# Retention and mixture of experts on one core: slot tables read ahead of weight pieces, squares moved up, later weight pieces issued around the second expert's column reads

## The chip, the cores and the metric

The kernel runs on one core of one Trainium2 chip. The metric is device time in microseconds (us) of one execution; lower is better. The kernel before takes 409.28 us, the median of 3 runs (408.39 to 411.97).

## What is computed

Two layers, one after the other. The first is a retention layer over 4 batches, 8 heads, 768 steps and 64 channels per head; the second routes each of the 3072 resulting rows of 512 numbers to one of 8 experts, a two-layer network with 1024 hidden units, and scales the result by the row's gate.

```python
for t in range(S):
    state = gamma[None, :, None, None] * state + np.einsum('bhd,bhe->bhde', k[:, :, t], v[:, :, t])
    y[:, :, t] = scale * np.einsum('bhd,bhde->bhe', q[:, :, t], state)
...
expert_idx = np.argmax(logits, axis=1)
...
h = np.maximum(x[mask] @ w1[e], 0.0)
out[mask] = gate_w[mask, None] * (h @ w2[e])
```

## The kernel before

The retention layer is worked in 12 blocks of 256 steps (12 is `NM`), and its rows go to DRAM (`xd`). For each row the routing picks an expert and a rank in it, and an indirect DMA on POOL writes the row's number, token and logits into that place of a slot table in DRAM (`tbl`, line 566). An expert works on the first rows of its part of the table: 416 rows for expert 0, down to 356 for the eighth (`CAPS`).

**Expert 0 starts before routing is finished.** Its first 288 slots, the early rows, are filled by block 8, so they are gathered (`xge`) and run through the first layer while the last blocks are still being placed. The other 128 slots, the late rows, can be read only when the last scatter of the slot table has landed: SP reads the slots (line 945, `tb[:, 0, 3]`), POOL gathers the rows they name (`xr0`, line 596), and TensorE turns them (line 1100). SP also reads the 512 slots of experts 1 and 2 (`slots`, line 913), for which it must first have the expert's number in a register (`load_expert`, line 178, a load of `cnti`).

**The rows of expert 1** take the long way that all later experts take: gathered by POOL in four indirect DMAs (`gather_rows`, line 596), written to DRAM by SP (`write_rows`: three DMAs of line 982 and one of line 986, each behind its own gather), and read back by columns in four DMAs (`read_quarters`, line 1001, `xg`; here called the column reads; 832 KB in all), which wait until all four writes have landed. DVE transposes what was read (`x_turn`, line 1011), ACT casts it to a high part, and DVE subtracts to get the low part (`x_low`, line 1018). TensorE needs both for expert 1's first layer (line 237).

**Weights come in pieces** of 512 KB, eight for each expert: four of the first layer's matrix (line 194), four of the second's (line 198). Piece g is loaded by `load_piece` into one of four buffers `raw`, so its load waits until piece g-4 has been split. `split` has ACT cast the piece to a high part `whi` (line 219) and DVE subtract to get the low part `wlo` (line 224). Every matrix product is done three times, high by high, high by low and low by high. Pieces 8 to 11 are the first layer of expert 1, pieces 12 to 15 its second layer. They are split in this order: piece 8 after the third tile of expert 0's second layer, 9 between the two halves of the late rows' first layer, 10 and 11 each behind one of the two turns of the late rows' hidden units (`turn_hidden`, lines 1138 and 1139).

**What sets the order.** Every engine works through its instructions in the order in which the program is written, and so does SP, whose queue carries all direct DMAs: an issue that waits holds up every issue behind it. `square` (line 278, ACT) sums the squares of a block of 128 rows for the gates. The POOL memset of `xr0` (line 1086) reuses memory of `xge`, so it waits for the squares of the early rows.

Of the kernel before, what the change touches and what calls it, by code (L numbers as in the profile page):

```python
# [32 lines left out]
NE = 8  # L33
# [6 lines left out]
CAPS = (416, 408, 400, 392, 384, 380, 360, 356)  # L40
# [5 lines left out]
EARLY = 288  # L46
EROWS = ((0, P), (1, P), (2, EARLY - 2 * P))
# [58 lines left out]
def retention_moe(ctx: ExitStack, tc: tile.TileContext, q, k, v, emb, tau, w1, w2, const, const16, out):  # L106
    nc = tc.nc
# [17 lines left out]
    tbl = dp.tile([NE * STRIDE, SW], F32, name="tbl")  # L125
# [12 lines left out]
    tb = cp.tile([P, NE, NG, 2 + NE], F32, name="tb")  # L138
# [35 lines left out]
    def after(i, o):  # L174
        tc.add_manual_dep(i.ins, o.ins.name, SYNC, reason="pace")

    def load_expert(s):
        expert[s] = nc.values_load(cnti[:, s:s + 1], engines=(ET.SP,), min_val=0, max_val=NE - 1)

    def load_piece(behind=None):  # L180
        g = nload[0]
        if g >= NPC:
            return
        nload[0] += 1
        s, j = divmod(g, 8)
        e = expert[s]
        r = rp.tile([P, 1024], F32, name="raw")
        if s == 0 and j < 4:

            for jj in range(KT):  # L190
                f = P * jj + Q * j
                nc.sync.dma_start(out=r[jj * Q:(jj + 1) * Q], in_=w1[0, f:f + Q, :])
        elif j < 4:
            i = nc.sync.dma_start(out=r, in_=w1r[ds(e * DM + j * P, P), :])
            if behind is not None:
                after(i, behind)
        else:
            i = nc.sync.dma_start(
                out=r.rearrange("p (c d) -> p c d", c=2),
                in_=w2r[ds(e * DF + 2 * (j - 4) * P, 2 * P), :].rearrange("(c p) d -> p c d", p=P))  # L200
            if behind is not None:
                after(i, behind)
        raw_t[g] = r

    def split_cast(parts=1):

        g = nsplit[0]
        if g >= NPC:
            return lambda *a: None
        nsplit[0] += 1  # L210
        r = raw_t.pop(g)
        hi = wp.tile([P, 1024], F32R, name="whi")
        lo = wp.tile([P, 1024], F32R, name="wlo")
        views = [t.rearrange("p (q t a) -> p q t a", q=8, t=4) for t in (r, hi, lo)]
        if g % 8 >= 4 and g // 8 not in ROWS:
            views[1:] = [t.rearrange("p (t q a) -> p q t a", q=8, t=4) for t in (hi, lo)]
        vs = [tuple(t[:, i * 8 // parts:(i + 1) * 8 // parts] for t in views) for i in range(parts)]
        for rv, hv, _ in vs:
            nc.scalar.copy(out=hv, in_=rv)  # L219
        piece[g] = (hi, lo)  # L220

        def low(*engs):
            for eng, (rv, hv, lv) in zip(engs or (nc.vector,) * parts, vs):
                eng.tensor_tensor(out=lv, in0=rv, in1=hv.bitcast(F32), op=ALU.subtract)  # L224
        return low

    def split(*engs):
        split_cast(len(engs) or 1)(*engs)
# [47 lines left out]
    def square(xr, n, j, at, e=0):  # L276
        sq = cp.tile([P, DM], BF16, name="sq")
        nc.scalar.activation(out=sq[:n], in_=xr[:n, j], func=AF.Square, accum_out=ssqs[e % 2][:n, at:at + 1])  # L278
# [39 lines left out]
    xge = ap_.tile([P, len(EROWS), DM], F32, name="xge", bufs=1)  # L318
# [442 lines left out]
    for m in range(NM):  # L761
# [16 lines left out]
        n = 2 if m < 7 else 3 if m < 8 else 4  # L778
# [44 lines left out]
        else:  # L823
# [6 lines left out]
            if m == 2:  # L830
                after(nc.sync.dma_start(
                    out=tbl.rearrange("(e s) c -> e (s c)", e=NE)[:, :FILL * SW].rearrange("e (p x) -> e p x", p=P // NE),
                    in_=none), i)
# [72 lines left out]
    def run(n):  # L906
        for _ in range(n):
            next(todo, None)

    def slots(e):  # L910
        if e not in expert:
            load_expert(e)
        nc.sync.dma_start(out=tb[:, e], in_=tbl[ds(expert[e] * STRIDE, NG * P), :2 + NE].rearrange("(j p) o -> p j o", p=P))
# [19 lines left out]
    for o in held:  # L933
        o()
    low()
    for _ in range(9):
        next(sort_steps)
        run(1)
    load_expert(1)
    load_piece()  # L940
    run(10)
    split()
    load_piece()
    load_expert(2)
    nc.sync.dma_start(out=tb[:, 0, 3], in_=tbl[EARLY:CAPS[0], :2 + NE])
    slots(1)
    slots(2)
    run(12)
    split()
    for j, n in EROWS:  # L950
        square(xge, n, j, j)
    run(12)
    split()
    load_piece()
    load_piece()
    run(DF)
    ctxa.close()
    turn_of[:] = ["b2", "b3"]
# [16 lines left out]
    def full_rest(e):  # L975
        return divmod(blocks_of(e) * Q, P)

    def write_rows(e):
        full, rest = full_rest(e)
        xr, xs = xrs[e], xsd[e % 2]  # L980
        for j in range(full if e == 1 else 0):
            nc.sync.dma_start(out=xs[j * P:(j + 1) * P], in_=xr[:, j])
        if e > 1:
            nc.sync.dma_start(out=xs[:full * P].rearrange("(j p) x -> p j x", p=P), in_=xr[:, :full])
        if rest:
            nc.sync.dma_start(out=xs[full * P:full * P + rest], in_=xr[:rest, full])

    def squares(e, part=None):
        full, rest = full_rest(e)
        sizes = [(j, P) for j in range(full)] + [(full, rest)] * (rest > 0)  # L990
        for j, n in sizes if part is None else sizes[2 * part:2 * part + 2]:
            square(xrs[e], n, j, j, e)
# [4 lines left out]
    def read_quarters(e):  # L997
        nb, xs = blocks_of(e), xsd[e % 2]
        xg = xgs[e] = mp.tile([P, NXC, P], F32, name="xg")
        for i in range(NQ):  # L1000
            nc.sync.dma_start(out=xg[i * Q:(i + 1) * Q, :nb],
                              in_=xs[:nb * Q, i * P:(i + 1) * P].rearrange("(n b) x -> b n x", b=Q))
# [3 lines left out]
    def x_turn(e, kt):  # L1006
        if kt == 0:
            xTs[e] = (hp.tile([P, KT, CAP], F32R, name="xh"), hp.tile([P, KT, CAP], F32R, name="xl"))
        xt = xts[e, kt] = mp.tile([P, NXC, Q], F32, name="xt", bufs=2)
        n = blocks_of(e)  # L1010
        nc.vector.transpose(out=xt[:, :n], in_=xgs[e][:, :n, kt * Q:(kt + 1) * Q])  # L1011
        nc.scalar.copy(out=xTs[e][0][:, kt, :CAPS[e]], in_=xt.rearrange("p n b -> p (n b)")[:, :CAPS[e]])  # L1012
# [98 lines left out]
    gsteps = gates(0, [(n, slice(j, j + 1), tb[:n, 0, j:j + 1, 2:]) for j, n in (*EROWS, (3, P))])  # L1111
    next(gsteps)
    write_rows(1)
    hr = mp.tile([P, DF], F32, name="hr")
    for f in (slice(0, 512), slice(512, 1024)):
        acc = acc_()
        n = 0
# [8 lines left out]
            squares(1, 0)  # L1126
            run_all(gsteps)
    read_quarters(1)
    load_piece()
    load_piece()  # L1130

    def turn_hidden(f):
        ps = pt_()
# [11 lines left out]
    turn_hidden(1)  # L1145
    split()
    squares(1, 1)
    load_piece()
    x_turn(1, 0)
    x_turn(1, 1)  # L1150
# [123 lines left out]
    with ExitStack() as cx:  # L1274
# [42 lines left out]
        with tc.If(any_over > 0):  # L1317
# [7 lines left out]
            for e in range(NE):  # L1325
                nc.gpsimd.indirect_dma_start(
                    out=tbl[:, :], out_offset=bass.IndirectOffsetOnAxis(ap=nxi[:, e:e + 1], axis=0),
                    in_=none, in_offset=None, bounds_check=NE * STRIDE - 1, oob_is_err=False)
# [31 lines left out]
```

## Time and profile before

| | |
|---|---|
| median of 3 runs | 409.28 us |
| the profiled execution | 409.33 us |
| its span, first to last instruction | 407.6 us |
| mean granted TensorE clock | 0.986 |
| TensorE (PE) busy | 392.3 us of the span |
| VectorE (DVE), ScalarE (ACT), GpSimd (POOL) busy | 254.2, 213.5, 154.8 us |
| DMA moved | 88.39 MB, mean 217 GB/s |

Times in the trace are microseconds from the start of the span. The engine called SP issues DMAs; a row of its timeline shows how long the issuing took, not the transfer. A line of the chain of waits names what the end was waiting for at that time; "issue" is time in which nothing that the profile shows was awaited. An idle time in square brackets names what ended it.

### The profile page before, as it was taken

Reading aid. Unit: us, or ns where it says so; the run is one execution under the profiler, and the core shown is the slowest. Engines: PE = TensorE matmul, PEld = TensorE weight load, DVE = VectorE, ACT = ScalarE, POOL = GpSimd, SP = SyncE. Lnnn points to the kernel's source line nnn. Section 1 sums busy time; section 2 is a strip of 40 time slices with the busy share of each in tenths; the row PEclk is TensorE's granted clock in tenths of the full one; section 3 lists DMA queues with packets and bytes.
Section 4 is the critical chain, followed back from the end, with each engine's and each line's share of the span. In section 5 each row is a group of like instructions: output and inputs, shape, how many; then the busy total and the mean of one; then the engine's idle time right before and its main releaser. Section 6 shows DMA issues by size and latency. Waiting matters only on the chain.

```text
span 407.6 us, 9526 instructions
## 1 busy us (share of the span) xinstructions
PE 392.3 (96%) x3646; PEld 359.1 (88%) x3646; DVE 254.2 (62%) x539; ACT 213.5 (52%) x378; POOL 154.8 (38%) x170
## 2 busy tenths in 40 slices
PE   7999999999899999999999999999999999999993
PEld 3998788878687998899999999999889889999972
DVE  5496877767489847871963676396266465586400
ACT  4565566545484627543745644565475365563410
POOL 2666477676333270701631330261274062000040
PEclk9999999999799999999999999999999999999997
DMA  8998979888437978879596896888969958934121
GB/s 233 266 291 255 270 218 261 238 220 245 112 81 189 277 233 198 282 222 276 187 297 166 254 301 197 233 280 248 257 242 329 206 183 247 247 127 126 32 98 53
DMA packets 88479, 88.39 MB, mean 217 GB/s; under 512 B 10808, under 2 KB 67000, under 8 KB 88424
## 3 DMA queue, kind: packets, MB, share of 16 engines
q1 hardware_dynamic: 83176, 74.60, 64.5%
q0 software_dynamic: 5072, 13.03, 9.4%
q8 instruction: 30, 0.49, 0.5%
q14 instruction: 25, 0.20, 0.1%
q10 hardware_dynamic: 176, 0.07, 0.1%
HBM read 65.01 MB, written 18.79 MB: 206 GB/s over the span
## 4 chain that ended last, share of the span: by engine, by line
PE 76%; DVE 6%; issue 6%; DMA 5%; SPq 4%; POOL 1%; ACT 1%; POOLq 0%; DVEq 0%; ACTq 0%
PE pst L237 11%; PE b L237 9%; PE py L237 8%; PE py L1030 8%; PE b L1030 6%; PE pst L1030 6%; PE py L444 5%; PE b L381 5%; PE b L1078 4%; PE py L1078 4%; PE pst L415 2%; SPq L1042 2%; PE b L350 2%; DMA tbl<-parts 2%; DVE x L468 2%
## 5 line engine op out<-in xcount | busy, mean ns | idle before, releaser
L224 DVE TENSOR_TENSOR wlo<-raw,whi 128x1024 fp32r<-128x1024 f32 x64 | 77.8, 1219 | 21.0 <-ACT whi L219 13.6
L1060 POOL DMA_INDIRECT out_dram<-og,si x28 | 30.4, 1086 | 125.1 <-ACT og L1053 88.7
L219 ACT CAST whi<-raw 128x1024 fp32r<-128x1024 f32 x64 | 66.2, 1044 | 2.1 <-DMA raw<-in_moe_w_dram 2.1
L1011 DVE STREAM_TRANSPOSE xt<-xg 128x384 f32<-128x384 f32 (+1 forms) x28 | 15.7, 579 | 34.1 <-DMA xg<-xs 33.9
L596 POOL DMA_INDIRECT xr<-xd,gi x24 | 29.9, 1244 | 17.2 <-ACT sq L278 9.9
L401 DVE TENSOR_TENSOR pm<-b,mask 128x512 f32<-128x512 f32 x48 | 29.8, 681 | 9.1 <-PE b L381 9.1
L344 POOL TENSOR_TENSOR hl<-wlo,cst 128x512 f32<-128x512 f32 x22 | 22.7, 1051 | 32.9 <-DMA wlo<-in_k_dram 20.9
L237 PE MATMUL pst<-xl,whi 128*128 128x380 f32 (+7 forms) x96 | 32.1, 335 | 0.2 <-issue 0.2
L237 PE MATMUL pst<-xh,whi 128*128 128x380 f32 (+7 forms) x96 | 32.0, 334 | 0.0
L237 PE MATMUL pst<-xh,wlo 128*128 128x380 f32 (+7 forms) x96 | 32.0, 333 | 0.0
L566 POOL DMA_INDIRECT tbl<-zt,sloti x24 | 24.4, 1018 | 19.2 <-DVE sloti L557 8.9
L381 PE MATMUL b<-qT,kT 64*128 64x128 f32 x384 | 27.9, 283 | 2.9 <-issue 2.0
L1012 ACT CAST xh<-xt 128x408 fp32r<-128x408 f32 (+6 forms) x28 | 14.3, 510 | 28.4 <-DVE xt L1011 27.4
L381 PEld LDWEIGHTS b<-qT,kT 64*128 64x128 f32 x384 | 24.0, 187 | 5.6 <-issue 3.8
L237 PE MATMUL py<-xl,whi 128*128 128x288 f32 (+7 forms) x80 | 26.3, 328 | 0.5 <-DVE xl L621 0.5
L237 PE MATMUL b<-xh,whi 128*128 128x408 f32 (+7 forms) x80 | 26.7, 334 | 0.0
L237 PE MATMUL b<-xl,whi 128*128 128x408 f32 (+7 forms) x80 | 26.7, 333 | 0.0
L237 PE MATMUL b<-xh,wlo 128*128 128x408 f32 (+7 forms) x80 | 26.6, 332 | 0.0
L237 PE MATMUL py<-xh,whi 128*128 128x288 f32 (+7 forms) x80 | 26.3, 329 | 0.0
L237 PE MATMUL py<-xh,wlo 128*128 128x288 f32 (+7 forms) x80 | 26.2, 328 | 0.0
L444 PE MATMUL py<-pm,vs 128*64 128x128 f32 x384 | 24.3, 277 | 0.3 <-DVE vs L394 0.3
L243 ACT ACTIVATE hh<-pst 128x380 fp32r<-128x380 f32 (+7 forms) x24 | 11.6, 484 | 23.8 <-PE pst L237 23.1
(222 smaller groups left out, 1036.5 us busy)
## 6 DMA issues: line engine op xcount, KB each, us to landing
raw<-in_moe_w_dram SPq DMA_DIRECT2D x60, 512.0 KB
whi<-in_q_dram SPq DMA_DIRECT2D x24, 256.0 KB
xd<-x SPq DMA_DIRECT2D x48, 128.0 KB
wlo<-in_k_dram SPq DMA_DIRECT2D x11, 512.0 KB
xs<-xr SPq DMA_DIRECT2D x6, 768.0 KB
whi<-in_v_dram SPq DMA_DIRECT2D x6, 512.0 KB
wlo<-in_v_dram SPq DMA_DIRECT2D x6, 512.0 KB
xg<-xs SPq DMA_DIRECT2D x16, 192.0 KB
```

What stands on the lines that cost most here:

```text
L219: nc.scalar.copy(out=hv, in_=rv)
L224: eng.tensor_tensor(out=lv, in0=rv, in1=hv.bitcast(F32), op=ALU.subtract)
L237: nc.tensor.matmul(acc[:, :w], a[:, f], x[:, kt, cols], start=(n == 0), stop=(n == 3 * KT - 1))
L344: return eng.tensor_tensor(out=ks_r[:, m % 3, s, h], in0=kin[m % 3][:, h, s], in1=w[:, h], op=ALU.mult)
L381: nc.tensor.matmul(psc[a][:, j], kTs[m][a * D:(a + 1) * D, j, u].rearrange("p s c -> p (s c)"), q_cols(m, a, j, u), start=True, stop=True, ...
L401: o.append(nc.vector.tensor_tensor(out=pm, in0=psc[a], in1=w, op=ALU.mult))
L444: nc.tensor.matmul(pys[m][u][o * D:(o + 1) * D, j], lhsT, rhs, start=first, stop=True, skip_group_check=True)
L566: i = nc.gpsimd.indirect_dma_start(out=tbl[:, :], out_offset=bass.IndirectOffsetOnAxis(ap=sloti[:, n:n + 1], axis=0), in_=zt[:, n], in_off ...
L596: return nc.gpsimd.indirect_dma_start(out=xr[:n, j, :], out_offset=None, in_=xd[:rows_, :], in_offset=bass.IndirectOffsetOnAxis(ap=gi[:n, ...
L1030: nc.tensor.matmul(acc[:, :c], a[:, f], x[:, kt, :c], start=(n == 0), stop=(n == 3 * FT - 1))
L1060: i = nc.gpsimd.indirect_dma_start(out=out[:, :], out_offset=bass.IndirectOffsetOnAxis(ap=si[:n, e, j:j + 1], axis=0), in_=og[:n, j, :], i ...
L1078: nc.tensor.matmul(acc[:s, :], x[:, kt, at], a, start=(n == 0), stop=(n == 3 * FT - 1))
```

## The change

On SP the late rows' slots are read right behind the last block's row writes, ahead of any weight piece, and expert 1's slots before piece 8. Piece 9 goes behind expert 1's row writes, and pieces 10, 11 and 12 behind its column reads. The number of loads before expert 1 is the same (pieces 8 to 15). On ACT the squares of the early rows stand behind the activations of the first two tiles of the first layer, where they stood behind the fifth. The order on TensorE, DVE and POOL stays.

```diff
--- before.py
+++ after.py
@@ -933,26 +933,20 @@
     for o in held:
         o()
     low()
+    for j, n in EROWS:
+        square(xge, n, j, j)
     for _ in range(9):
         next(sort_steps)
         run(1)
+    nc.sync.dma_start(out=tb[:, 0, 3], in_=tbl[EARLY:CAPS[0], :2 + NE])
     load_expert(1)
-    load_piece()
-    run(10)
-    split()
+    slots(1)
     load_piece()
     load_expert(2)
-    nc.sync.dma_start(out=tb[:, 0, 3], in_=tbl[EARLY:CAPS[0], :2 + NE])
-    slots(1)
     slots(2)
-    run(12)
-    split()
-    for j, n in EROWS:
-        square(xge, n, j, j)
-    run(12)
-    split()
-    load_piece()
-    load_piece()
+    for _ in range(3):
+        run(12)
+        split()
     run(DF)
     ctxa.close()
     turn_of[:] = ["b2", "b3"]
@@ -1111,6 +1105,7 @@
     gsteps = gates(0, [(n, slice(j, j + 1), tb[:n, 0, j:j + 1, 2:]) for j, n in (*EROWS, (3, P))])
     next(gsteps)
     write_rows(1)
+    load_piece()
     hr = mp.tile([P, DF], F32, name="hr")
     for f in (slice(0, 512), slice(512, 1024)):
         acc = acc_()
@@ -1126,8 +1121,8 @@
             squares(1, 0)
             run_all(gsteps)
     read_quarters(1)
-    load_piece()
-    load_piece()
+    for _ in range(3):
+        load_piece()
 
     def turn_hidden(f):
         ps = pt_()
@@ -1145,6 +1140,7 @@
     turn_hidden(1)
     split()
     squares(1, 1)
+    load_piece()
     load_piece()
     x_turn(1, 0)
     x_turn(1, 1)
```

SP behind the last block's row writes, as it was (`cnti` is the experts' numbers, raw_2356 and raw_2375 are pieces 8 and 9, the tb of line 945 is the late rows' slots, the tb of line 913 those of expert 1):

```order
L178 TENSOR_LOAD cnti_77
L178 ISA x2
L194 ISA
L194 DMA raw_2356<-in_moe_w1_dram 128x1024
L194 ISA
L194 DMA raw_2375<-in_moe_w1_dram 128x1024
L178 TENSOR_LOAD cnti_77
L178 ISA x2
L945 DMA tb_78<-tbl_67 128x10
L913 ISA
L913 DMA tb_78<-tbl_67 128x4x10
```

and as it is now (raw_2364 is piece 8):

```order
L941 DMA tb_78<-tbl_67 128x10
L178 TENSOR_LOAD cnti_77
L178 ISA x2
L913 ISA
L913 DMA tb_78<-tbl_67 128x4x10
L194 ISA
L194 DMA raw_2364<-in_moe_w1_dram 128x1024
L178 TENSOR_LOAD cnti_77
L178 ISA x2
L913 ISA
L913 DMA tb_78<-tbl_67 128x4x10
```

The three slot reads have gone ahead: the late rows' in front of everything, expert 1's in front of piece 8, and piece 9 is no longer here.

SP around the column reads, as it was (raw_2434 and raw_2436 are pieces 10 and 11, raw_2659 is piece 12, xs the row writes, xg the column reads):

```order
L194 ISA
L194 DMA raw_2434<-in_moe_w1_dram 128x1024
L194 ISA
L194 DMA raw_2436<-in_moe_w1_dram 128x1024
L982 DMA xs1_66<-xr_2476 128x512 x3
L986 DMA xs1_66<-xr_2476 32x512
L1001 DMA xg_2654<-xs1_66 32x13x128 x4
L198 ISA
L198 DMA raw_2659<-in_moe_w2_dram 128x2x512
```

and as it is now (raw_2598 is piece 9, raw_2655 and raw_2657 are pieces 10 and 11):

```order
L976 DMA xs1_66<-xr_2470 128x512 x3
L980 DMA xs1_66<-xr_2470 32x512
L194 ISA
L194 DMA raw_2598<-in_moe_w1_dram 128x1024
L995 DMA xg_2650<-xs1_66 32x13x128 x4
L194 ISA
L194 DMA raw_2655<-in_moe_w1_dram 128x1024
L194 ISA
L194 DMA raw_2657<-in_moe_w1_dram 128x1024
L198 ISA
L198 DMA raw_2659<-in_moe_w2_dram 128x2x512
```

Three pieces that stood in front of the column reads now stand among the row writes and behind the column reads.

ACT during expert 0's first layer, as it was (hh are the activations of the tiles, sq the squares):

```order
L243 ACTIVATE hh_2217<-py0_2237 128x288
L243 ACTIVATE hh_2217<-py1_2276 128x288
L243 ACTIVATE hh_2217<-pst0_2290 128x288
L243 ACTIVATE hh_2217<-pst1_2335 128x288
L219 CAST whi_2371<-raw_2052 128x8x4x32
L243 ACTIVATE hh_2217<-b0_2367 128x288
L219 CAST whi_2405<-raw_2233 128x8x4x32
L278 ACTIVATE sq_2409,ssq0_81<-xge_121 128x512
L278 ACTIVATE sq_2411,ssq0_81<-xge_121 128x512
L278 ACTIVATE sq_2413,ssq0_81<-xge_121 32x512
L243 ACTIVATE hh_2217<-b1_2401 128x288
L219 CAST whi_2430<-raw_2235 128x8x4x32
```

and as it is now:

```order
L243 ACTIVATE hh_2217<-py0_2237 128x288
L243 ACTIVATE hh_2217<-py1_2276 128x288
L278 ACTIVATE sq_2319,ssq0_81<-xge_121 128x512
L278 ACTIVATE sq_2321,ssq0_81<-xge_121 128x512
L278 ACTIVATE sq_2323,ssq0_81<-xge_121 32x512
L243 ACTIVATE hh_2217<-pst0_2290 128x288
L243 ACTIVATE hh_2217<-pst1_2341 128x288
L219 CAST whi_2392<-raw_2052 128x8x4x32
L243 ACTIVATE hh_2217<-b0_2386 128x288
L219 CAST whi_2411<-raw_2233 128x8x4x32
L243 ACTIVATE hh_2217<-b1_2405 128x288
L219 CAST whi_2430<-raw_2235 128x8x4x32
```

The three squares have moved up past two casts and three activations.

## Rows read from the trace of the kernel before

**Rows 1.** The page, part 1: busy time, share of the span, instructions.
```profile
PE 392.3 (96%) x3646; PEld 359.1 (88%) x3646; DVE 254.2 (62%) x539; ACT 213.5 (52%) x378; POOL 154.8 (38%) x170
```

**Rows 2.** The chain that ended last, 118 to 185 us: start, length, what.
```profile
158.93 0.44 PE b L1136 x4
...
164.95 1.29 PE pst L237 x7
...
166.40 1.35 PE pst L237 x5
167.76 4.43 PE b L237 x24
```

**Rows 3.** Timeline of POOL, 100 to 190 us: start, length, work, idle before.
```profile
107.01 0.97 POOL L566 DMA_INDIRECT tbl<-zt,sloti  x1 [0.30 <-issue]
112.24 1.13 POOL L596 DMA_INDIRECT xge<-xd,tb  x1 [4.26 <-issue]
...
133.91 1.23 POOL L566 DMA_INDIRECT tbl<-zt,sloti  x1 [0.30 <-issue]
138.79 0.53 POOL L1086 MEMSET xr<- 128x512 f32 x1 [3.65 <-ACT sq L278]
143.90 1.16 POOL L596 DMA_INDIRECT xr<-xd,tb  x1 [4.59 <-DMA tb<-tbl]
...
145.68 1.11 POOL L596 DMA_INDIRECT xr<-xd,gi  x1 [0.28 <-POOL gi L590]
```

**Rows 4.** Timeline of SP's DMA queue, 100 to 190 us: issue start, length, transfer.
```profile
109.43 0.39 SPq L602 DMA_DIRECT2D tb<-tbl  x1
...
137.48 1.00 SPq L194 DMA_DIRECT2D raw<-in_moe_w_dram  x2
139.20 0.34 SPq L945 DMA_DIRECT2D tb<-tbl  x1
...
149.39 3.65 SPq L982 DMA_DIRECT2D xs<-xr  x3
153.51 0.32 SPq L986 DMA_DIRECT2D xs<-xr  x1
155.99 1.88 SPq L1001 DMA_DIRECT2D xg<-xs  x4
158.07 4.53 SPq L198 DMA_DIRECT2D raw<-in_moe_w_dram  x4
```

**Rows 5.** Windows of 2 us: five engines' busy time, clock, DMA share, GB/s.
```profile
158.00:160.00 2.00, 2.00 (x16) 1.86 (x15) 1.74 (x2) 1.43 (x3) 0.00 (x0) 1.00 1.23 206
160.00:162.00 2.00, 2.00 (x10) 1.60 (x9) 1.75 (x3) 1.97 (x4) 0.00 (x0) 1.00 1.16 210
162.00:164.00 2.00, 2.00 (x10) 1.63 (x9) 1.76 (x4) 1.34 (x4) 0.93 (x1) 1.00 1.04 386
```

**Rows 6.** Timeline of ACT, 116 to 190 us.
```profile
131.67 0.41 ACT L243 ACTIVATE hh<-py 128x288 fp32r<-128x288 f32 x1 [2.58 <-PE pst L237]
...
136.32 0.63 ACT L278 ACTIVATE sq<-xge 128x512 bf16<-128x512 f32 x1
...
153.04 1.04 ACT L219 CAST whi<-raw 128x1024 fp32r<-128x1024 f32 x1
...
157.77 1.07 ACT L219 CAST whi<-raw 128x1024 fp32r<-128x1024 f32 x1
...
159.89 1.05 ACT L219 CAST whi<-raw 128x1024 fp32r<-128x1024 f32 x1
```

**Rows 7.** Timeline of DVE, 116 to 190 us.
```profile
135.26 0.45 DVE L246 SCALAR_TENSOR_TENSOR hl<-pst,hh 128x288 fp32r<-128x288 f32 x1
...
160.03 0.69 DVE L1139 TENSOR_TENSOR hl<-b,hh 128x512 fp32r<-128x512 f32 x1
160.97 1.23 DVE L224 TENSOR_TENSOR wlo<-raw,whi 128x1024 fp32r<-128x1024 f32 x1 [0.25 <-ACT whi L219]
162.34 1.10 DVE L1011 STREAM_TRANSPOSE xt<-xg 128x416 f32<-128x416 f32 x2
```

## The prediction

> **What bounds the kernel now.** I read the page's first part, then the chain of waits around the change, then the timelines of the engines that feed TensorE there, and last the DMA rate in windows of 2 us. TensorE is busy for 392.3 of 407.6 us [rows 1], so a gain has to come out of a gap on TensorE. In the stretch that the change touches (about 132 to 168 us) the chain is TensorE itself, with one gap. The first tile of expert 1's first layer has 12 products. Seven of them start at 164.95, the other five only at 166.40, and the next tile at 167.76 [rows 2]; that next tile does 24 products in 4.43 us, so 12 take 2.21 us. The first tile took 2.81, and 0.6 us of that is waiting.
>
> For what? DVE's low part of piece 11 starts at 160.97, and behind it come the transposes of expert 1's columns at 162.34, which TensorE needs [rows 7]. DVE is late there because TensorE's second turn of the late rows' hidden units comes at 158.93 [rows 2], ACT casts piece 11 behind it at 159.89 [rows 6], and DVE follows ACT. So the gap of 0.6 us hangs on TensorE's own order, not on a DMA, and the change does not touch that order. The late rows, whose slots the change reads earlier, leave no gap that the chain shows. So the most that can be won in this execution is about 0.6 us, and what can be lost is whatever pieces 10 and 11 come late.
>
> **The squares.** The three squares are not new, they only move. They begin at 136.32 with 0.63 us each [rows 6] and are over by 138.79, when the memset that they release begins [rows 3]: at most 2.5 us. Now they start behind the second tile's activation, which begins at 131.67 and takes 0.41 [rows 6], and end by 134.6. The third tile's activation follows and is done by 135.0; DVE wants it at 135.26 [rows 7]. The casts behind it were to wait for the squares anyway, one later than now. Cost 0; the cover is 0.3 us, and what is missing of it would delay the low part of piece 7, not TensorE at once. The memset can now run up to 4 us earlier.
>
> **The slot reads.** The last scatter of the slot table starts on POOL at 133.91, and the late rows' gather at 143.90, 4.7 us behind the slot read that SP issued at 139.20 [rows 3, 4]. In front of that read stand pieces 8 and 9, 1 MB, from 137.48 on. The trace has the same two steps on an almost idle DMA: scatter at 107.01, read issued at 109.43, gather at 112.24 [rows 3, 4], so 2.4 us from scatter to landing and 2.8 from read to gather. For the first step the other end is 3.7 us, as from expert 1's first gather at 145.68 to the write that waited for it at 149.39. So the read goes out at 136.3 to 137.6, and the late rows' gather starts at 139.1 to 140.4. Expert 1's first gather stood 1.78 us behind it (143.90 to 145.68) and I keep that, as its slots are read right behind the register load: 140.9 to 142.2, which is 4.8 to 3.5 us earlier. TensorE wanted nothing earlier, so this alone is worth 0. Behind the first slot read wait the register load, expert 1's slots, piece 8, the second load and expert 2's slots. Piece 8 is cast only behind the late rows' turn, one cast ahead of the one at 153.04 [rows 6], so its delay of about a microsecond is hidden.
>
> **The pieces.** Here a price can arise. Row writes began at 149.39, the last at 153.51, the column reads at 155.99 [rows 4]. With the gathers 4.8 to 3.5 us earlier the last write is at 148.7 to 150.0, piece 9 right behind it, and the column reads begin at 151.2 to 152.5. Piece 9 is cast at 153.04 [rows 6], some 3 to 4 us behind its issue, and ACT has room behind it; I take 0.
>
> Pieces 10 and 11 are issued behind the column reads, at about 153.2 to 154.5; before, they were issued ahead of the row writes. When do they land? In the trace, pieces 12 and 13 were issued behind the column reads from 158.07 on [rows 4]. The rate stayed at 206 and 210 GB/s until 162, and only then rose to 386 [rows 5]. 832 KB at 208 GB/s take 4.1 us, so until 162 the DMA engines did column reads and the pieces stood behind them. That is 6.0 us from the first column read's issue (155.99) to the end of the last one. The change gives 157.2 to 158.5 for that end. Piece 10 follows at 386 GB/s in 1.4 us, piece 11 in another 1.4: 158.6 to 159.9 and 160.0 to 161.3, with 0.3 us to be seen (162.0 to 162.34 for the transposes).
>
> Piece 10 was cast at 157.77; now 158.9 to 160.2, so 1.1 to 2.4 us late. DVE does the low part of piece 10, then the low part of the late rows' hidden units (160.03, 0.69 us), then the low part of piece 11 [rows 7]; all slide. Piece 11's cast, with the turn's cast ahead of it, is ready by then. The transposes slide from 162.34 by the same 1.1 to 2.4 us, and so does the end of TensorE's wait, one for one, since TensorE already waits there. Pieces 12 and 13 come earlier, 14 and 15 with the splits of 10 and 11; nothing waits for them near.
>
> Both ends of the piece term: 0 or a gain of up to the 0.6 us that TensorE waits, if pieces and column reads share the DMA engines and the gathers, now beside fewer pieces, land faster; 2.4 us if the slot table lands late. I take 1.1, the end where the scatter lands as at 107, since from 138 on the ring is now nearly empty.
>
> The Trainium skill, page "DMA: Bandwidth & Descriptors", section "Anatomy of one DMA — SWDGE (gpsimd) path", fits a DMA of POOL's kind as 2.0 us plus its bytes at 436 GB/s. By it a piece would land 3.2 us behind its issue, piece 10 at about 156.4, piece 11 at 156.9, and the sum would be 0. It counts nothing that stands ahead in the queue; the windows of rows 5 speak for the queue, and I go by them.
>
> **The sum.** Profiled execution 409.33 us; squares 0; slot reads 0; pieces +1.1: 410.4 us. The profiled execution stands 0.05 us above the median of the runs shown, so I leave it at 410.4.
>
> **Rivals.**
> - *Hidden.* Pieces 10 and 11 land in time for 157.77 and 159.89. For it: in this stretch DMA has room, and gathers beside fewer weights may land sooner than in 3.7 us; 1.1 us is all that is needed. Against it: rows 5. Time: 409.3. The skill's fit above gives the same.
> - *A small gain.* The late rows now have some 4 us more before TensorE turns them. In the profile they come in time, but the runs reach from 408.39 to 411.97, and a run in which they come late would show a wait at that turn. With that gone, and at best the 0.6 us of rows 2: 408.7. Against it: the profiled execution is as long as the median and has no such wait.
> - *The slots do not come earlier, and the pieces pay.* If the gathers of expert 1 keep their place (the read waits for the scatter longer than I think, or the small reads stay slow), the column reads begin at 155.99 as before, end at 162.0, piece 10 is there at 163.7, and the transposes slide by 5.9 us: 415.2. Each microsecond of the 4.8 that is lost costs one; over 1% (4.1 us) from 3.0 lost on, that is, if expert 1's first gather starts later than 143.9. For it: a DMA of small slots took 4.7 us once. Against it: that one had 1 MB ahead of it.
> - *No effect of the order.* That SP waited for something else at these places, so that nothing moves, is excluded for the pieces, since their issue behind the column reads is in the program.
>
> **How the numbers follow.** Forecast (0.3 to 2.4 us slower) 0.50, hidden 0.27, small gain 0.12, slots not earlier 0.11. The forecast's own range is 409.6 to 411.8. For 8 in 10 the range has to take in hidden and most of the small gain, and part of the last rival: 408.3 to 413.0. One per cent is 4.1 us, about what a measurement of this kernel can tell from no change. Slower by more than that needs the last rival nearly whole: 0.08. Faster by more needs 4.1 us out of a stretch with 0.6 us of waits: 0.02. Within it: 0.90.
>
> **What would show it.** In the trace after: the late rows' gather on POOL at about 139 to 140 in place of 143.90; row writes from about 144.6 on; column reads at about 151; piece 10's cast at about 158.9 with an idle time ended by the piece's DMA; the transposes at about 163.4; and 1.7 us lost in the first tile of expert 1 in place of 0.6. If piece 10's cast stands at 157.8 with no DMA wait, the piece term is wrong and the time is 409.3 or below. If column reads begin at 154 or later, the slot term is wrong and the time is above 412.

## The result and the profile after

The changed kernel takes 411.12 us, the median of 12 runs (409.09 to 413.72). The kernel before took 408.83 us (12 runs). The ratio is 1.0065, with a 95% interval of 1.004 to 1.009, so the change costs about 2.7 us (1.6 to 3.7). The profiled execution took 411.29 us with a span of 409.6. The time forecast, 410.4 us, lies 0.7 us below the median, and the range holds it; but the forecast's own step was +1.1 us, and that lies below the interval. That the time came so near is in part luck: the step was 1.2 us short of the medians' difference of 2.3, and the forecast started from 409.3, 0.5 us above the median of the 12 runs before.

TensorE has not more work, only more waiting. The page's first part, which answers to [rows 1]:

```profile
PE 393.5 (96%) x3646; PEld 359.8 (88%) x3646; DVE 253.9 (62%) x539; ACT 213.2 (52%) x378; POOL 150.3 (37%) x170
```

The profiled executions differ by 1.96 us (411.29 against 409.33), and that is a sum of two opposite things. This execution reached expert 0's second layer 0.89 us sooner, for reasons outside the change: at 120 us, ahead of everything that was moved, its chain of waits already stands 0.90 us earlier (products of line 506 at 119.89, before 120.79). So I count from the first product of that layer, "the start" from here on: 139.27 us before, 138.38 after. Counted from there, the second tile of expert 1 begins at 28.33 us before (167.60) and at 31.24 after (169.62): 2.91 us later. 2.91 less 0.89 is 2.02, which is the 1.96 to within 0.06 us: what comes after that tile takes as long as before. In all twelve profiles used here, from expert 1's second tile to the end of the span it takes 239.9 to 240.0 us.

Timeline of TensorE in the kernel before, at the start and at expert 1's second tile (start, length, work):

```profile
139.27 0.30 PE L1030 MATMUL pst<-hh,whi 128*128 128x288 f32 x1
...
167.60 0.35 PE L237 MATMUL b<-xh,whi 128*128 128x408 f32 x1
```

The same view of the kernel after, with the idle time ahead of an instruction and what ended it in brackets:

```profile
138.38 0.30 PE L1024 MATMUL pst<-hh,whi 128*128 128x288 f32 x1
...
157.50 0.29 PE L1024 MATMUL py<-hh,wlo 128*128 128x288 f32 x1
158.18 0.66 PE L1131 MATMUL b<-ident,hr 128*128 128x128 f32 x4 [0.38 <-ACT hr L1118]
158.65 0.50 PE L1072 MATMUL pst<-whi,hh 128*128 128x512 f32 x1
159.38 0.50 PE L1072 MATMUL pst<-whi,hl 128*128 128x512 f32 x1 [0.22 <-DVE hl L1134]
...
162.03 0.46 PE L1072 MATMUL pst<-whi,hh 128*128 128x512 f32 x1
163.37 0.50 PE L1072 MATMUL pst<-whi,hl 128*128 128x512 f32 x1 [0.87 <-DVE hl L1134]
...
169.62 0.35 PE L237 MATMUL b<-xh,whi 128*128 128x408 f32 x1
```

There are three new holes. The first two stand at 158.18 and 159.38, around the second turn of the late rows' hidden units. The third, the largest, is at 163.37. The gap that was there before, in expert 1's first tile, has grown: the tile lasts 3.59 us from its first product at 166.03 where it took 2.81. Together these are some 0.2 us more than 2.91, because a small wait of the kernel before is gone: there TensorE's turn of the late rows (line 1100) began at 148.29, 0.35 us behind the product ahead of it, and now it follows in 0.13 (147.18 behind 147.05).

The waits lead back to the weight pieces. ACT in the kernel after, the casts of pieces 9, 10 and 11 (compare [rows 6], where none of them waits):

```profile
153.75 1.05 ACT L219 CAST whi<-raw 128x1024 fp32r<-128x1024 f32 x1 [1.74 <-DMA raw<-in_moe_w_dram]
...
157.54 0.58 ACT L1118 ACTIVATE hr<-py 128x512 f32<-128x512 f32 x1
...
160.41 1.05 ACT L219 CAST whi<-raw 128x1024 fp32r<-128x1024 f32 x1 [1.81 <-DMA raw<-in_moe_w_dram]
...
161.83 1.05 ACT L219 CAST whi<-raw 128x1024 fp32r<-128x1024 f32 x1
```

ACT waited 1.74 us for piece 9 and 1.81 us for piece 10. Behind piece 9's cast stands `hr`, the late rows' hidden units that TensorE turns at 158.18. (It comes 3.8 us behind the cast, as before, because between them ACT waits for DVE's gates, and these stand behind piece 9's low part.) So an ACT that waits for a weight holds up rows of the other expert. From the last scatter to piece 10 the chain of waits now runs mostly through DMAs, where in [rows 2] it was TensorE:

```profile
132.94 4.69 DMA tbl<-zt,sloti
...
137.65 1.54 DMA tb<-tbl
...
145.83 3.58 DMA xr<-xd,gi
...
149.42 1.61 DMA xs<-xr
...
153.31 7.07 DMA raw<-in_moe_w_dram
...
160.41 1.06 ACT whi L219
...
163.23 1.22 DVE wlo L224
164.44 0.53 DVE xt L1005
...
169.78 4.43 PE b L237 x24
```

It reads: the last scatter of the slot table landed 4.69 us after it started, the slot read went out, the last gather took 3.58 us, the last row write 1.61; then came the column reads, and piece 10, issued behind them at 153.31, was in only 7.07 us later. This is the row on which the result rests.

SP's queue and POOL show that the slot part did what it was made for. SP after, which answers to [rows 4]:

```profile
137.65 0.35 SPq L941 DMA_DIRECT2D tb<-tbl  x1
...
146.14 2.30 SPq L976 DMA_DIRECT2D xs<-xr  x3
149.42 0.32 SPq L980 DMA_DIRECT2D xs<-xr  x1
150.04 0.34 SPq L194 DMA_DIRECT2D raw<-in_moe_w_dram  x1
151.21 1.88 SPq L995 DMA_DIRECT2D xg<-xs  x4
153.31 0.93 SPq L194 DMA_DIRECT2D raw<-in_moe_w_dram  x2
```

POOL after, which answers to [rows 3]:

```profile
132.94 1.23 POOL L566 DMA_INDIRECT tbl<-zt,sloti  x1 [0.30 <-issue]
138.30 0.53 POOL L1080 MEMSET xr<- 128x512 f32 x1 [4.14 <-DMA xd<-x]
139.98 1.06 POOL L596 DMA_INDIRECT xr<-xd,tb  x1 [1.15 <-DMA tb<-tbl]
...
141.79 1.11 POOL L596 DMA_INDIRECT xr<-xd,gi  x1 [0.43 <-POOL gi L590]
```

Windows of 2 us after, as in [rows 5]: the last two numbers are the DMA share and GB/s.

```profile
132.00:134.00 2.00, 2.00 (x18) 2.00 (x17) 1.90 (x6) 1.97 (x7) 1.70 (x2) 1.00 1.00 254
...
138.00:140.00 2.00, 2.00 (x18) 2.00 (x17) 2.00 (x4) 0.41 (x1) 0.55 (x2) 1.00 0.04 3
...
154.00:156.00 2.00, 2.00 (x17) 2.00 (x16) 1.17 (x2) 1.97 (x5) 0.00 (x0) 1.00 0.94 194
156.00:158.00 2.00, 1.80 (x14) 1.56 (x12) 1.50 (x12) 0.77 (x4) 0.00 (x0) 1.00 1.20 196
158.00:160.00 2.00, 1.60 (x8) 1.14 (x9) 0.93 (x3) 0.60 (x2) 0.00 (x0) 1.00 1.01 382
```

The engines are full at 132, when the scatter starts, and empty at 138; from 154 to 158 they move the column reads at some 195 GB/s with a share of about 1, and only from 158 on the rate of weight pieces, 382.

### The profile page after: what moved, and what is told of

Read it like the earlier page. It is cut to its first block, busy times and chain, and to the rows that moved or that the text cites. A ratio compares the mean times of both kernels' runs of the same rounds, so it can differ in the third digit from the quotient of the medians.

```text
span 409.6 us, 9526 instructions
## 1 busy us (share of the span) xinstructions
PE 393.5 (96%) x3646; PEld 359.8 (88%) x3646; DVE 253.9 (62%) x539; ACT 213.2 (52%) x378; POOL 150.3 (37%) x170
## 4 chain that ended last, share of the span: by engine, by line
PE 66%; DVE 11%; DMA 7%; issue 7%; SPq 4%; POOL 2%; ACT 1%; POOLq 0%; DVEq 0%
PE pst L237 10%; PE b L237 8%; PE py L237 8%; PE py L1024 7%; PE b L1024 5%; PE py L444 5%; PE b L381 4%; PE pst L1024 4%; PE b L1072 4%; PE py L1072 4%; SPq L1036 2%; PE pst L415 2%; DVE vs L394 2%; DVE x L468 2%; DMA raw<-in_moe_w_dram 2%
## 5 line engine op out<-in xcount | busy, mean ns | idle before, releaser
L1054 POOL DMA_INDIRECT out_dram<-og,si x28 | 29.4, 1049 | 121.2 <-ACT og L1047 86.5
L596 POOL DMA_INDIRECT xr<-xd,gi x24 | 28.6, 1192 | 20.4 <-issue 18.2
L263 POOL TENSOR_TENSOR r<-r,half 128x4 f32<-128x4 f32 (+1 forms) x9 | 8.9, 991 | 49.9 <-DVE r L262 49.9
```

Of the source, the lines that this page charges most:

```text
L596: return nc.gpsimd.indirect_dma_start(out=xr[:n, j, :], out_offset=None, in_=xd[:rows_, :], in_offset=bass.IndirectOffsetOnAxis(ap=gi[:n, ...
L1054: i = nc.gpsimd.indirect_dma_start(out=out[:, :], out_offset=bass.IndirectOffsetOnAxis(ap=si[:n, e, j:j + 1], axis=0), in_=og[:n, j, :], i ...
```

## The experiments

The experiments ran on chips on which the kernel before takes 401.7 or 401.8 us, so only ratios are compared with the result above; the changed kernel itself was not run on those chips. "Expert 1's second tile" is always told from the start defined above. It tells of one execution, while a ratio is of medians: in some kernels below the two differ by 1 to 2 us, so a few tenths of a microsecond in a single profile prove little. Theory Q says that the pieces issued behind the column reads come late because they stand behind them in the queue. Its rivals: that one of the other two parts of the change costs the time (E, the early slot reads; S, the squares), that piece 9 does (N), or that the column reads themselves are late. The expectations call the loss 2.3 us, the difference of the medians.

### The parts by themselves

Only the squares moved, all else as before:

```diff
     low()
+    for j, n in EROWS:
+        square(xge, n, j, j)
     for _ in range(9):
...
-    for j, n in EROWS:
-        square(xge, n, j, j)
```

> The kernel before with the squares of the early rows moved up and nothing else. Theory Q (queue): ratio 0.999 to 1.001, the low part of the third tile's activation on DVE waits for nothing new, and the memset of the late rows' buffer starts earlier while the late rows' gather does not. Theory S (the squares hold up ACT, and what run e4 lost comes from them): ratio 1.002 to 1.003.

Measured: ratio 1.0006 (0.9985 to 1.0026), and expert 1's second tile at 28.34 us against 28.33. The squares cost nothing, as the forecast had it.

Only the slots of the late rows and of expert 1 read ahead of the weight pieces, all else as before:

```diff
+    nc.sync.dma_start(out=tb[:, 0, 3], in_=tbl[EARLY:CAPS[0], :2 + NE])
     load_expert(1)
+    slots(1)
     load_piece()
...
     load_expert(2)
-    nc.sync.dma_start(out=tb[:, 0, 3], in_=tbl[EARLY:CAPS[0], :2 + NE])
-    slots(1)
     slots(2)
```

> The kernel before with one edit: the late rows' slots and expert 1's slots are read ahead of piece 8; all pieces keep their place ahead of the row writes, the squares keep theirs. Theory Q (the loss comes from pieces 9 to 11 standing behind row writes and column reads in SP's queue): no loss, ratio 0.998 to 1.001 to the kernel before, 0.6 us lost in expert 1's first tile as before, and the late rows' gather about 3 us earlier than 143.9. Theory E (the loss comes from the early part: slot reads ahead, gathers that now meet other transfers): 410 to 411.5 us, ratio 1.003 to 1.007.

Measured: ratio 1.0011 (0.9987 to 1.0035). The late gather starts 2.14 us after the start (before 4.63), so it is 2.5 us earlier; yet the first column read goes out at 16.48 (before 16.72). The lead is lost in between: from expert 1's first gather to the first row write, which waits for it, it takes 7.45 us where it took 3.71. The last section comes back to it. Expert 1's second tile stands at 28.88 us, 0.55 later than before, as DVE waits 0.48 us for the column reads.

Only the pieces in their new places, with the slot reads put back behind piece 8 and both register loads (the squares moved too, at no cost):

```diff
-    nc.sync.dma_start(out=tb[:, 0, 3], in_=tbl[EARLY:CAPS[0], :2 + NE])
     load_expert(1)
-    slots(1)
     load_piece()
     load_expert(2)
+    nc.sync.dma_start(out=tb[:, 0, 3], in_=tbl[EARLY:CAPS[0], :2 + NE])
+    slots(1)
     slots(2)
```

> The changed kernel with the slot reads put back behind piece 8 and the register loads; pieces 9 to 12 stay behind the row writes and the column reads. Theory Q: the slot reads come later by what piece 8 takes of the DMA engines, 1.4 to 2.5 us; column reads and piece 10 slide with them, and the loss against the kernel before rises from 2.3 us to 4 to 5.5 us, ratio 1.010 to 1.014. Theory I (reading the slots early brings nothing, what counts is the pieces' place alone): ratio 1.0065 as for the changed kernel.

Measured: ratio 1.0109 (1.0071 to 1.0147), and expert 1's second tile at 32.35 us, 4.02 later than before. With the slots read early it is 2.91. So the pieces' places cost the time. The early slot reads give about 1.1 us of it back by the profiles (the intervals of the ratios overlap), with the column reads starting at 12.83 us in place of 14.17. Alone, the early slots are worth nothing; in these runs they pay only where the pieces have been put behind the reads that they bring forward.

### Which piece

The kernel after without the load of piece 9, with piece 8's data split in its place:

```diff
     write_rows(1)
-    load_piece()
+    raw_t[nload[0]] = keep[nload[0] - 1]
+    nload[0] += 1
```

> The changed kernel without the load of piece 9: piece 8's data is split in its place, so the work on every engine is the same and only 0.5 MB of DMA is gone, which stood between the row writes and the column reads. Theory Q: piece 9's cast waits for no DMA; the column reads and piece 10 land 1 to 1.5 us earlier, and the loss against the kernel before falls to 0.8 to 1.6 us, ratio 1.002 to 1.004. Theory N (piece 9 was the cause, and piece 10 late only behind it): ratio 1.000, piece 10's cast without a wait.

Measured: ratio 1.0042 (1.0026 to 1.0059). Expert 1's second tile is at 31.07 us, 0.17 earlier than with piece 9. The two holes of together about 1 us that piece 9 makes on TensorE are gone, and in this execution it helps next to nothing, since the wait for piece 10 grows by 1.70 us (ACT in this kernel):

```profile
152.06 1.05 ACT L220 CAST whi<-raw 128x1024 fp32r<-128x1024 f32 x1 [3.51 <-DMA raw<-in_moe_w_dram]
```

The cast waits 3.51 us where it waited 1.81. Piece 10 is hardly earlier (its cast is at 21.86 us against 22.03 in the kernel after), where I had expected 1 to 1.5 us; whatever TensorE lost ahead of it is part of that wait. But in this execution the column reads also went out 0.65 us later (13.48 against 12.83). By the ratios, 1.0042 against 1.0065, piece 9 may cost some 0.9 us, with intervals that overlap. So its price by itself, 0.2 us by the one and 0.9 by the other, stays open.

The kernel after without the loads of pieces 10 and 11 (piece 9's data are split in their place), and one without 9, 10 and 11 (piece 8's data), which has the edit for piece 9 above as well. The edit of the first:

```diff
     read_quarters(1)
-    for _ in range(3):
-        load_piece()
+    for _ in range(2):
+        raw_t[nload[0]] = keep[9]
+        nload[0] += 1
+    load_piece()
```

> The kernel after, without the loads of pieces 10 and 11: piece 9's data are split in their place, so the output is not the reference's; piece 9 stays where the change put it. Theory Q (TensorE's loss in expert 1's first tile is the wait for piece 10 behind the column reads, and piece 9's gap of 1.05 us is hidden behind it as long as piece 10 is later): the second tile of expert 1 starts 29.2 to 29.6 us from the start of expert 0's second layer (before 28.33 plus 1.05; after 31.24), ratio 1.001 to 1.004. Rival (the column reads themselves land too late, whatever pieces stand behind them): about 30.5 to 31.2, ratio 1.005 to 1.007, and the transposes wait for the column reads.

> The kernel after, without the loads of pieces 9, 10 and 11: piece 8's data are split in their place, so the output is not the reference's. Theory Q: no wait for pieces is left; the second tile of expert 1 starts at 27.7 to 28.4 us from the start of expert 0's second layer (before 28.33), ratio 0.998 to 1.001. Rival (the column reads themselves land too late): 30 or more, ratio 1.004 or more.

Measured without 10 and 11: expert 1's second tile at 27.82 us, 0.51 before the place that it has in the kernel before, ratio 1.0018 (0.9997 to 1.004). Without all three: 27.87 us, ratio 0.999 (0.9962 to 1.0018). The column reads go out at 11.61 and 12.98 us (after 12.83), and the transposes do not wait for them: DVE without pieces 10 and 11 takes them right behind piece 11's low part.

```profile
156.50 1.23 DVE L225 TENSOR_TENSOR wlo<-raw,whi 128x1024 fp32r<-128x1024 f32 x1
157.64 1.10 DVE L1006 STREAM_TRANSPOSE xt<-xg 128x416 f32<-128x416 f32 x2
```

So the loss is the wait for the pieces, and the rival that blames the column reads falls: without the three pieces the reads go out as late as in the kernel after, and nothing is lost. In the profile pieces 10 and 11 alone account for all of the 2.91 us, but there the reads went out 1.2 us earlier. I had expected 29.2 to 29.6 us where only 10 and 11 are missing, because piece 9 should then show its hole. In that execution it made none: the scatter landed sooner, the slot read went out 1.89 us ahead of the start (0.73 after), and piece 9 was issued at 9.93 us in place of 11.66. So ACT waits for piece 9 in one execution and not in another. The measured ratio of 1.0018 lies 1.2 us above what that profile says; whether piece 9 explains it stays open.

### Other places for the pieces

Piece 9 back ahead of the row writes, 10 to 12 behind the column reads:

```diff
     for i in range(3):
         run(12)
         split()
+        if i == 0:
+            load_piece()
...
     write_rows(1)
-    load_piece()
```

> The changed kernel with piece 9 put back ahead of the row writes; 10 to 12 stay behind the column reads. Theory Q: the cast of piece 9 waits for no DMA, the waits of TensorE for the late rows' first hidden units (about 1 us) are gone, and the column reads have 0.5 MB less ahead of them, so that piece 10 lands up to 1.4 us earlier; the loss falls from 2.3 us to between 0.5 and 1.5 us, ratio 1.001 to 1.004. Theory N (piece 9 alone makes the loss): ratio 1.000. Theory E: no change against the changed kernel, ratio 1.0065.

Measured: ratio 1.0058 (1.0032 to 1.0084), worse than I expected, with expert 1's second tile at 32.39 us in the profile. ACT no longer waits for piece 9. But issued beside the gathers it slows them: from the first gather to the first row write 6.39 us, where the kernel after has 4.35. The column reads start at 14.84 us in place of 12.83, and piece 10's cast waits 4.83 us.

Pieces 10 and 11 between piece 9 and the column reads:

```diff
+    load_piece()
+    load_piece()
     read_quarters(1)
-    for _ in range(3):
-        load_piece()
+    load_piece()
```

> The changed kernel with pieces 10 and 11 issued between the row writes (and piece 9) and the column reads, instead of behind the column reads. Theory Q: the casts of 10 and 11 wait for no DMA; the column reads end about as late as pieces 10 and 11 did, near 162 us of the changed kernel's time, and the transposes of expert 1 begin 0.3 to 1 us later than in the kernel before; piece 9's waits of about 1 us stay. Ratio 1.002 to 1.004. Theory N: as the changed kernel, 1.0065. Theory E: 1.0065.

Measured: ratio 1.0077 (1.0045 to 1.0109), as bad as the change itself, and missed too; expert 1's second tile is at 30.94 us. No cast waits for piece 10 or 11 now. In their place the column reads are late (DVE, with its idle time before):

```profile
160.47 1.10 DVE L1005 STREAM_TRANSPOSE xt<-xg 128x416 f32<-128x416 f32 x2 [1.70 <-DMA xg<-xs]
```

The transposes stand at 25.68 us from the start, against 25.98 after and 23.07 before. Whoever is last in the queue is waited for.

All of pieces 9, 10 and 11 ahead of the row writes, as before, with the slots early and the squares moved:

```diff
     for _ in range(3):
         run(12)
         split()
+        load_piece()
```

> The changed kernel with pieces 9, 10 and 11 back ahead of the row writes: what is left of the change are the slot reads ahead, the squares moved up and pieces 12 and 13 where they were. Theory Q: no loss, ratio 0.998 to 1.001, and the column reads land some 3 us earlier than in the kernel before without TensorE gaining from it, because the transposes wait in DVE's order behind the low part of piece 11. Theory E: as the changed kernel, 1.0065.

Measured: ratio 1.0024 (1.0001 to 1.0047), above what I expected, with expert 1's second tile at 28.94 us. No piece is waited for; the column reads are, by 0.99 us. They go out not 3 us earlier than before but at 17.19 us, 0.47 later. Its chain of waits shows where the early slots' lead went:

```profile
136.86 7.60 DMA xr<-xd,gi
...
144.88 2.85 DMA xs<-xr
...
149.30 4.89 DMA xg<-xs
...
154.38 0.62 DVE xt L1006
```

The third of expert 1's four gathers takes 7.60 us, where the chain of the kernel after has the fourth with 3.58, and the last row write 2.85 where it has 1.61.

Last, the kernel with only the slots early, and expert 2's slots read behind the column reads, so that they too are out of the way:

```diff
     load_expert(1)
     slots(1)
     load_piece()
...
-    load_expert(2)
-    slots(2)
...
     read_quarters(1)
+    slots(2)
```

> Run e1 (slots of the late rows and of expert 1 ahead of the pieces) with the slots of expert 2 read behind the column reads, where they are early enough for expert 2's gather. Theory Q: the gathers of expert 1 have one transfer of small packets less beside them, the row writes and column reads come 0.5 to 1.2 us earlier than in e1, DVE's wait for the column reads (0.5 us in e1) goes; ratio to the kernel before 0.998 to 1.001. Rival: the 512 small packets cost nothing, the column reads stand where they stood in e1.

Measured: ratio 1.0033 (1.0006 to 1.006). Its profile shows what theory Q said: the column reads go out at 15.33 us (16.48 with expert 2's slots ahead), DVE does not wait for them, and expert 1's second tile is 0.38 us earlier than before. Yet the runs are 1.3 us slower (0.2 to 2.4). The gathers are not faster without the small packets (7.74 us to the first row write, against 7.45); they start 1.13 us earlier. POOL waits 8.70 us for expert 2's slots, but that is not the price: expert 2's first gather starts at 23.64 us, before at 23.80. Where the 1.3 us go stays open. None of the kernels that load all pieces beats the one before.

## Why the prediction came out as it did

**The squares: right.** Cost 0, and the runs with the squares alone say 0. The memset of the late rows' buffer, though, did not move up by the 4 us that it might have: it stands at 138.30, 0.08 us ahead of the start, where it stood 0.48 ahead. The profile puts its wait down to a write of rows to DRAM ("4.14 <-DMA xd<-x"), and in other runs to other work, so what it waits for stays open. The late gather behind it waits longer for its slots anyway.

**The slot reads: right in what they do, a little late.** To compare places I add 0.89 us to the times of after. The step from scatter to landing was 4.7 us where I had bounds of 2.4 and 3.7. I had taken the better end because the DMA would be nearly empty, but the scatter starts at 132.94, when the engines are full (a share of 1.00); they are empty only once it has landed (3 GB/s from 138 to 140). The step from read to gather was 2.3 (2.8 forecast), and the two gathers stood 1.81 apart (1.78). So the late gather was at 140.9 (139.1 to 140.4 forecast), expert 1's first at 142.7 (140.9 to 142.2), the last row write at 150.3 (148.7 to 150.0) and the first column read at 152.1, inside its 151.2 to 152.5. That the late rows come in time in the kernel before was not quite right: TensorE waited some 0.2 us for them (148.29), and with the earlier gather that wait is gone.

**The pieces: right in mechanism, wrong in size.** The term was +1.1 us, with ends of a gain and of +2.4; it measured 2.9 in the profiles, beyond its end, and 2.7 by the ratio. The failed step is the landing of piece 10. I had its cast at 158.9, with the column reads at the early end of their range; it was at 161.3 (160.41 plus 0.89), 2.4 us later. That is made, to about half a microsecond in each term that a window's edge enters, of: 0.9 us because the column reads began at 152.1 and not at 151.2; 0.8 because the DMA engines left the rate of about 195 GB/s only some 6.8 us after the first read's issue (158 less 151.21) and not 6.0; 1.0 because piece 10 landed 2.4 us after that and not 1.4; less 0.3 that I had left between landing and cast. For the 0.8 the runs name a cause: piece 9, whose load had been put right in front of the reads. Without it, piece 10's cast came 8.4 us after the first column read (21.86 less 13.48) in place of 9.2 (22.03 less 12.83). Windows of 0.5 us show it in the kernel after: while the first reads are issued, the engines still move at the rate of pieces, and the rate of the reads ends only behind 158.

```profile
151.50:152.00 0.50, 0.50 (x4) 0.41 (x3) 0.00 (x0) 0.50 (x1) 0.40 (x2) 1.00 0.95 369
152.00:152.50 0.50, 0.50 (x4) 0.41 (x3) 0.00 (x0) 0.01 (x1) 0.00 (x0) 1.00 1.00 393
...
157.50:158.00 0.50, 0.30 (x3) 0.06 (x1) 0.30 (x2) 0.50 (x2) 0.00 (x0) 1.00 0.93 184
158.00:158.50 0.50, 0.33 (x3) 0.33 (x4) 0.24 (x2) 0.50 (x2) 0.00 (x0) 1.00 0.98 319
```

The 1.0 is not settled. At the rate of the window, some 0.9 MB moved between 158.0 and 160.38, nearly two pieces, so piece 10 did not have the engines to itself; I had counted one piece at full rate and no time for the transfer's completion.

Here the fit in the Trainium skill, "DMA: Bandwidth & Descriptors", section "Anatomy of one DMA — SWDGE (gpsimd) path", which the prediction weighed, stands at an estimated 3.2 us for a piece. It is a fit for DMAs issued by POOL, and these are issued by SP. The trace has 7.07 us from issue to landing behind the column reads. The fit counts nothing that stands ahead in the queue, as the prediction said; the queue decided. The same section puts most of its fixed 2.0 us behind the last byte, in the confirmation of the write. My 1.4 us for piece 10 left out any such time, and its 2.4 fits that, but no run separates the two.

**Piece 9: taken as 0, wrong in place, its effect not settled.** I saw that its cast stood 3 to 4 us behind its issue and took that as enough. It was not in this execution: piece 9 was issued at 150.9 (150.04 plus 0.89), the cast of the kernel before stood at 153.04, and the cast now begins 3.71 us behind the issue. ACT waited 1.74 us, and that made two holes of together about 1 us on TensorE. Without it the loss fell by only 0.17 us in the profile, where a hole ahead of a larger wait for the same queue did not add to it; by the ratios it may be 0.9.

**From the cast to TensorE.** "One for one" held at its end: the transposes are 2.91 us later and so is expert 1's second tile. Of the 3.5 us by which the cast of piece 10 slid, 0.6 was taken up on the way to the transposes, where ACT had waited 0.57 us for TensorE (159.41 in the kernel before) and now does not. The place was told wrongly, though: I expected 1.7 us lost in expert 1's first tile, where 0.6 had been lost. That tile lost 1.4 (3.59 less 2.21). The rest stands ahead of it, about half of it at 163.37, because the low part of the late rows' second half of hidden units waits on DVE behind piece 10's low part. I had written that order of DVE down and had not followed it to TensorE.

**The rivals.** "Hidden" and "a small gain" fall with piece 10's wait of 1.81 us. "The slots do not come earlier, and the pieces pay" is what the run with only the pieces moved did, with +4.0 us; I had priced it at 5.9, because I took the column reads to stay where they were, and they came 2.5 us earlier there too, with fewer pieces in front of the slot reads and the gathers.

## What to carry to other kernels

Where a stretch's transfers fill the DMA engines, moving one ahead of another does not remove a wait, it chooses who is last; before such a move, write down for each transfer when its data are needed, and put the bulk load whose data are needed first ahead of the small-row reads, not behind them. Price a load behind a strided read by the time in which that read drains, which the trace's windows show, and not by its own bytes. And a gap on the chain can be worth less than its length when the next wait comes from the same queue: take away the load itself, and see what is left.

## What the runs showed that I had not expected

Gathers issued by POOL slowed down when pieces of weights were issued by SP beside them, though they are on another queue. From expert 1's first gather to the first row write it took 3.7 us in the kernel before and 4.35 after (3.65 to 4.98 in the six other kernels with no more pieces beside the gathers), but 6.39 with one more piece issued beside the gathers, and 7.4 to 7.9 in the three kernels that issue pieces 9, 10 and 11 just ahead of the gathers or among them (the two with the slots early and the pieces as before, and the one with all pieces ahead). The windows of the kernel with all pieces ahead show what went over the engines meanwhile, and what they did with the column reads later:

```profile
138.00:140.00 2.00, 2.00 (x18) 2.00 (x17) 0.00 (x0) 0.07 (x1) 1.24 (x3) 1.00 0.98 352
140.00:142.00 2.00, 2.00 (x13) 1.81 (x13) 1.59 (x4) 2.00 (x5) 0.00 (x0) 1.00 1.01 389
...
150.00:152.00 2.00, 2.00 (x12) 1.72 (x11) 1.86 (x2) 1.42 (x3) 0.00 (x0) 1.00 1.23 204
152.00:154.00 2.00, 2.00 (x10) 1.64 (x9) 1.23 (x1) 1.48 (x5) 0.00 (x0) 1.00 1.14 216
```

From 138 to 142 the engines move up to 389 GB/s, the rate of weight pieces, while the gathers are waited for. The Trainium skill, "DMA: Bandwidth & Descriptors", section "Queues, rings and completion order", says that an engine takes turns between the queue rows that it has work for, a packet at a time; a gather would then share the engines with SP's pieces as long as there are any. The rows agree in that pieces move while the gathers are waited for; the taking of turns itself is seen in no run. With the column reads the engines are just as busy (a share of 1.14 to 1.23) at 204 to 216 GB/s, about half the rate. By these rates, as an estimate, the 832 KB of column reads cost the engines as much time as some 1.5 MB of pieces (832 KB times 385 over 208), and that is what pieces 10 and 11 stood behind in the changed kernel.
